# A gated mix of linear and softmax attention: branch A's normalising steps gathered into one iteration

## The chip, the cores and the metric

The kernel runs on one core of a Trainium2 chip. The core's engines work side by side: TensorE (PE, with its weight loads as PEld) for matrix products, VectorE (DVE), ScalarE (ACT) and GpSimd (POOL) for the rest, and SyncE (SP), whose queue issues the DMA transfers. Each engine works through its own list of instructions in order, and semaphores tie the lists together. The metric is the device time of one execution in microseconds (us), and the time given for a kernel is the median of its runs.

## The reference

The input x is 2048 tokens by 448 numbers, with 16 heads of 28 numbers each. Two attention branches are computed on the same x and mixed by a gate for each token:

```
g = sigmoid((x * gate_w).sum(-1))
out = g * A(x) + (1 - g) * B(x)

A: q, k, v = split(x @ wqkv); pq, pk = q @ w_phi, k @ w_phi         (per head)
   phi_q = [softmax(pq), softmax(-pq)]; phi_k = [softmax(pk), softmax(-pk)]
   kv = phi_k^T v; z = sum(phi_k); num = phi_q kv; den = phi_q z + 1e-6
   A = (num / den) @ wo
B: A = softmax(q k^T / sqrt(28)) v @ wo
```

So branch A is a linear attention with 56 features a head, and branch B a full softmax attention over all pairs of tokens.

## The kernel before, in words

Many factors of products are kept in two parts, a high part (the number rounded to TensorE's input format, F32R) and a low part (what the rounding left), and such a product is made in three passes. Tokens are tiled by 128, which gives 16 tiles; branch A's queries are also taken in 8 blocks of 256.

The program has three stretches. One loop of 44 iterations i computes branch A's keys, values and queries, and much of what branch B needs. After it branch B's attention runs block by block over all pairs, and then the results are joined. The change lies in the last half of that loop. There t = i is the tile of keys and values, q = i - 16 that of queries, y = q - 1 the step that A's output is at, and tb = y // 2 its block.

A block b of branch A takes these steps. `numer` makes its numerators and denominators on PE. `normalize1` copies the numerators from PSUM to a tile `oU` (ACT, L418) and gathers the denominators by a DMA (L420). `normalize2` adds the epsilon (DVE, L426), takes the reciprocals (L427), sends them to DRAM (L430) and spreads them over the partitions by four broadcast DMAs (L435). `normalize3` is the normalising product `oU * rs` (DVE, L441, 128x1024). `normalize4` makes the high parts (ACT, L448, two of 128x512) and the low parts (L449): the first by POOL, the second by DVE. `take_spread` then moves rows within the tile `oT` by four DMAs (L461), since `out_a` takes the output product in passes that need some rows in the partitions that stood empty. `out_a` (PE, tile `poa`) makes the output of one tile of tokens, and `out_a2` multiplies it by the gate (ACT, L638, tile `ga`) and sends it to DRAM (L639). In the iterations: numer(b) at y = 2b + 4, normalize2 at y = 2b + 5, normalize3 at y = 2b + 8, normalize4 and the moves at y = 2b + 9, out_a for the two tiles at y = 2b + 11 and 2b + 12.

Around these stand other steps of the same iterations. `mx_unit` is a unit of branch B's row maxima: PE multiplies keys and queries into two PSUM tiles `pmb` and `pmd` (L296), ACT copies the one (L303, tile `rl`), and DVE takes the maximum of both (L305, two instructions). Its PSUM tiles have two buffers up to y = 20, so that a unit's products wait until ACT and DVE have done with an earlier unit; from then on three buffers. `features1` and `features2` make the softmax features of the queries (DVE L476, L477, L492, L493; POOL L480, L482, L494; ACT L474, L485), `turn` transposes them on PE (`pft`, L558) and copies them from PSUM (ACT, L561, tile `fT`). The first three tiles of branch B's values are computed early, while A's are still running, into tiles `ve0` and `ve1`, which use buffers of the row-max copies (tags rl2 and rl3). At q = NT + 6, which is y = 21, two DMAs copy them (L921, L922; 512 KB and 256 KB) into the value tile `vb0`. Two iterations later row-max copies may use the buffer rl2 again, and so have to wait for that transfer.

PE, DVE, ACT and POOL run in the order in which the program is written. SP's order is set by a scheduler, except that transfers wrapped in `kept()` keep the order in which they are written among themselves. SP issues in order: a transfer that waits holds all those behind it.

Of the kernel before, what the change touches and what calls it, by code (L numbers as in the profile page):

```python
# [24 lines left out]
NT = S // P  # L25
# [10 lines left out]
def f32(ap):  # L36
    return ap.bitcast(F32)
# [3 lines left out]
def gated_mix_kernel(ctx, tc, xT, wqkB, wvB, wvA, wkAT, wqAT, phi, woA, woB,  # L41
# [7 lines left out]
    nc = tc.nc  # L49
# [124 lines left out]
    def take_acts():  # L174
        while acts:
            acts.pop(0)()

    def take_subs():
        while subs:
            subs.pop(0)()  # L180
# [229 lines left out]
    def kept(x, n=2):  # L410
        if n == 2:
            tc.stamp_issue_order_token(x.ins, "turns")
# [10 lines left out]
    def normalize2(pool, oU, den, nm, n, eps):  # L423

        if eps:
            nc.vector.tensor_scalar_add(den, den, EPS)  # L426
        nc.vector.reciprocal(den, den)  # L427
        rd = dr.tile([4, n * 512], F32, tag=f"rd{n}", name=f"rd{nm}", bufs=2)
        rs = pool.tile([P, n, 512], F32, tag="rs", name=f"rs{nm}", bufs=2)
        kept(nc.sync.dma_start(rd, den), n)  # L430
        if n == 1:
            nc.sync.dma_start(rs[:, 0, :], rd.unsqueeze(1).to_broadcast([4, 32, 512]))
            return oU, rs
        for j in range(4):
            kept(nc.sync.dma_start(rs[32 * j:32 * j + 32].rearrange("p n q -> p (n q)"),  # L435
                                   rd[j:j + 1].to_broadcast([32, n * 512])))
        return oU, rs

    def normalize3(oU, rs, n):

        (nc.gpsimd if n == 1 else nc.vector).tensor_mul(oU, oU, rs)  # L441
        return oU

    def normalize4(pool, oU, nm, n):

        o = pool.tile([P, n, 2, 512], F32R, tag="oT", name=f"oT{nm}", bufs=2)
        for k in range(n):
            (nc.scalar.copy if n == 2 else nc.gpsimd.tensor_copy)(o[:, k, 0, :], oU[:, k, :])  # L448
            (nc.vector if n == 2 and k == 1 else nc.gpsimd).tensor_sub(  # L449
                o[:, k, 1, :], oU[:, k, :], f32(o[:, k, 0, :]))  # L450
        if n == 2:
            spread.append(o)
        return [o[:, k] for k in range(n)]
# [3 lines left out]
    def take_spread():  # L457
        while spread:
            o = f32(spread.pop())
            for r in range(0, P, 32):  # L460
                kept(nc.sync.dma_start(  # L461
                    o[r + DH:r + 32].rearrange("p k i n -> p (k i n)")[:, :1792].rearrange(
                        "p (s n) -> p s n", n=256),
                    o[r:r + DH, 1, 1, 256:]))
# [34 lines left out]
    def take_exps(left=0):  # L499
        while len(exps) > left:  # L500
            exps.pop(0)()

    fk, va, fq, fT_of, num, oTs = {}, {}, {}, {}, {}, {}
# [108 lines left out]
    def load_split(w, nm):  # L612
        for i in range(2):
            nc.sync.dma_start(f32(w[:, i, :, :D]), w_d[nm][:, i])
# [21 lines left out]
    def out_a2(t):  # L636
        ga = ta.tile([P, D], F32, tag="ga", name=f"ga{t}", bufs=2)
        nc.scalar.mul(ga, po_of.pop(t)[:, :D], gate[:, t:t + 1])  # L638
        nc.sync.dma_start(ga_d[t // 4][:, t % 4], ga)  # L639
# [167 lines left out]
    for i in range(2 * NT + 12):  # L807
        t, q = i, i - NT
        y = q - 1
        tb = y // 2  # L810
        take_acts()
        if t < NT and t % 2 == 0:
            mx_unit()
            passes = (55 if t < NT - 4 else 44) + (4 if t >= 4 else 0)
            pace["n"] = 4 if t >= 4 else 0
            pace["at"] = [passes // 3, 2 * passes // 3] if t <= 10 else [passes // 2]
        if q in (0, 1):
            take_exps()
        if part_low:
            part_low.pop()()  # L820
        if q == 0:
            woA_s = weights(3, "woA_s")
            wvB_s = weights(2, "wvB_s")
            load_split(woA_s, "woA")
            load_split(wvB_s, "wvB")

        if t % 2 == 0 and 0 <= t - 4 < NT:
            kv_add(t - 4)
            kv_add(t - 3)
        if q == 2:  # L830
            bk_s.close()
            ta_s = ExitStack()
            ta = ta_s.enter_context(tc.tile_pool(name="ta", bufs=1, reuse_waits="tile"))
            KV = ta.tile([P, 512], F32, name="KV")
            woC_s = ta.tile([P, 2, D], F32R, name="woC_s")
            woC0 = wqA_s.rearrange("p i b n -> p (i b) n")[:, :7, D:]
            nc.sync.dma_start(f32(woC_s), w_d["woA"][:, 0, 1:3])
            nc.sync.dma_start(f32(woC0), w_d["woA"][:, 0, 0].rearrange("p (a n) -> p a n", n=64))
            kvT = kv_copy()
            early = [ta.tile([P, 2 - i, 512], F32, tag=f"rl{i + 2}", name=f"ve{i}", bufs=1) for i in range(2)]  # L840
            early = [e.rearrange("p t (h d) -> p t h d", d=32) for e in early]
            for e in early:
                nc.gpsimd.memset(e[:, :, :, 28:], 0.0)
                nc.gpsimd.memset(e[:, :, :, 28:29], 1.0)
            turn4.append("")
            take_exps()
        if t < NT:
            pk = ps_s(f"pk{t}")
            tok_major(pk, t, wkA_s, D, tick)
            fk[t] = features1(pk, f"k{t}", nc.gpsimd)  # L850
            take_exps(1)
        if 0 <= q < NT:
            pq = ps_s(f"pq{q}")
            tok_major(pq, q, wqA_s, D)
        if q == 0:
            fk[NT - 1] = features2(fk[NT - 1], f"k{NT - 1}")
        if q in (1, 2):
            fq[q - 1] = features2(fq[q - 1], f"q{q - 1}")
        if 0 <= q < NT:
            fq[q] = features1(pq, f"q{q}", nc.vector if 0 < q < 11 else nc.gpsimd)  # L860
        if 0 <= t - 1 < NT - 1:
            fk[t - 1] = features2(fk[t - 1], f"k{t - 1}")
        if 8 <= q < 11:
            value_b(q - 8)
        if q == NT + 5:
            ps_s_.close()
            ps = ps_s_.enter_context(tc.tile_pool(name="psv", bufs=1, space=PSUM, reuse_waits="tile"))
            psn[:] = 2, 3
            turn4.clear()
        if q == NT + 8:  # L870
            rl_at[:] = [(rlp, "rl"), (ta, "rl2")]
        if q in (0, 1) or q >= 11:
            mx_unit()
        if y >= 9 and y % 2 and tb - 4 < 8:
            oTs[tb - 4] = normalize4(ta, num.pop(tb - 4), f"a{tb - 4}", 2)
            take_spread()
        if y >= 4 and y % 2 == 0 and tb - 2 < 8:
            numer(tb - 2)
        if q > 0:
            take_exps(int(q < NT))  # L880
        if q == 3:
            kv_out(kvT)
        if q in (4, 5):
            spare_weights(q - 4)
        if 2 <= q - 1 < NT:
            fq[q - 1] = features2(fq[q - 1], f"q{q - 1}")
        take_subs()
        if t == 1:
            pair_load(0, 3)
        if y >= 8 and y % 2 == 0 and tb - 4 < 8:  # L890
            num[tb - 4] = normalize3(*num[tb - 4], 2)
        if t < NT:
            value_a(t)
            if t % 2 and t < NT - 4:
                proj_qk(NP + t // 2, ev)
                if t < 8:
                    part_low.append(part_high(t // 2))
        if q in (0, 1):
            proj_qk(NP + 6 + q, ev)
        take_lows()  # L900
        if 2 <= i < 6:
            fold(wqA_s, "q", i - 2)
        if q == 1:
            ev_s.close()
        if q == 1:
            gates()
        if y < 9 or y % 2:
            if y >= 2 and y - 2 < NT:
                turn(y - 2)
        if 0 <= y - 11 < NT:  # L910
            out_a(y - 11)
            out_a2(y - 11)
        if y >= 9 and y % 2 == 0 and y - 2 < NT:
            turn(y - 2)
        if q == NT + 2:
            bd_s.close()
            vb = [value_tile(0)]
        if q == NT + 6:
            for e in early:
                nc.gpsimd.memset(e[:, 0, 0:1, 29:30], 0.0)  # L920
            nc.sync.dma_start(vb[0][:, 0:2], early[0])  # L921
            nc.sync.dma_start(vb[0][:, 2:3], early[1][:, 0:1])  # L922
        if q - NT in (3, 4, 6, 7, 9):
            value_b(3 + (3, 4, 6, 7, 9).index(q - NT), (lambda i: i == 5 and mx_unit()) if q >= NT + 5 else None)
        if y >= 5 and y % 2 and tb - 2 < 8:
            num[tb - 2] = normalize2(ta, *num[tb - 2], f"a{tb - 2}", 2, True)
    rl_at.clear()
    ta_s.close()
    wp_s.close()
# [445 lines left out]
```

## Time and profile before

| | us |
|---|---|
| median of 3 runs | 1001.29 |
| their range | 1001.2 to 1002.0 |
| the profiled execution's own time | 1001.51 |
| its span in the profile | 999.7 |
| PE busy in the span | 991.4 |
| ACT busy | 807.4 |
| DVE busy | 666.3 |
| POOL busy | 231.7 |

The span is what the profiler sees between the first and the last instruction; 1.8 us of the profiled execution lie around it. The clock that TensorE was granted was 0.999 of full speed. Rows of the profile's views give a start and a duration in us, the engine, the line of the kernel, the operation, the tiles that it writes and reads, and in brackets how long the engine had been idle before it and what ended that. L12 is line 12 of the kernel. PE has the longest busy time, and the loop that the change touches lasts until about 331 us.

### The profile page before, as it was taken

To read this page: it belongs to the slowest core of one execution; us is meant where nothing else is said; L and a number is where in the kernel's file an instruction comes from. 1 tells how busy PE (TensorE), PEld (TensorE's weight loads), DVE (VectorE), ACT (ScalarE), POOL (GpSimd) and SP (SyncE) were. 2 spreads that over 40 slices of the span, in tenths; PEclk is the share of its full clock that TensorE was granted. 3 is DMA by queue.
4 is the path that set the end of the run, shared out by engine and by line. 5 is a ranking of instruction groups with operands and counts; after the bars stand their busy time and mean duration, and the time that the engine had idled before them with its cause. 6 is when DMAs were issued, how large, how long until landed. Compare 5 with 4: busy or idle time off the path is not lost.

```text
span 999.7 us, 18087 instructions
## 1 busy us (share of the span) xinstructions
PE 991.4 (99%) x6456; PEld 553.5 (55%) x6456; DVE 666.3 (67%) x1343; ACT 807.4 (81%) x1532; POOL 231.7 (23%) x214
## 2 busy tenths in 40 slices
PE   9999999999999999999999999999999999999998
PEld 8878878887777533333333333333334444455656
DVE  6567666888764588878888788888886544444202
ACT  5445555568855899999999999999999999979672
POOL 1265455668415111110120100102001011101010
PEclk9999999999999999999999999999999999999999
DMA  8976312412445732332524324443233354216231
GB/s 291 316 243 211 121 59 78 169 46 79 119 131 133 163 96 56 78 79 64 114 58 108 81 51 142 90 99 94 59 90 77 76 113 120 51 37 148 62 106 56
DMA packets 69170, 109.09 MB, mean 109 GB/s; under 512 B 18216, under 2 KB 29112, under 8 KB 69080
## 3 DMA queue, kind: packets, MB, share of 16 engines
q1 hardware_dynamic: 69080, 107.94, 40.0%
q8 instruction: 51, 0.84, 0.4%
q14 instruction: 39, 0.32, 0.1%
HBM read 74.33 MB, written 31.45 MB: 106 GB/s over the span
## 4 chain that ended last, share of the span: by engine, by line
PE 95%; DMA 2%; SPq 1%; DVE 1%; issue 1%; ACT 0%; POOL 0%; POOLq 0%; DVEq 0%; ACTq 0%
PE st L1040 28%; PE pv L1144 25%; PE pm L337 9%; PE pqk L118 6%; PE pva L136 4%; PE pk L136 4%; PE pq L118 4%; PE pob L118 3%; PE pvb L136 2%; PE poa L118 2%; PE pmb L296 2%; PE pft L558 1%; PE pqk L725 1%; PE pkv L512 1%; DMA oTa<-oTa 1%; PE poL L1182 1%
## 5 line engine op out<-in xcount | busy, mean ns | idle before, releaser
L1043 ACT ACTIVATE p<-st 128x512 f32<-128x512 f32 x1020 | 527.2, 638 | 25.9 <-PE st L1040 25.9
L348 DVE TENSOR_REDUCE part<-pm 128x1 f32<-128x512 f32 x450 | 287.3, 685 | 150.5 <-PE pm L337 150.5
L1040 PE MATMUL st<-qst,kst 128*128 128x512 f32 x1020 | 301.0, 423 | 0.4 <-DVE acc L1159 0.4
L1144 PE MATMUL pv<-p,vb 128*32 128x512 f32 x2048 | 263.7, 602 | 0.0
L1040 PEld LDWEIGHTS st<-qst,kst 128*128 128x128 f32 x1020 | 168.7, 187 | 99.6 <-ACT p L1043 45.0
L341 ACT ACTIVATE rl<-pm 128x512 f32<-128x512 f32 x200 | 124.3, 622 | 13.9 <-PE pm L337 12.4
L337 PEld LDWEIGHTS pm<-kc,qc 28*128 28x128 f32 x800 | 38.2, 181 | 167.7 <-issue 101.4
L441 POOL TENSOR_TENSOR oUb<-oUb,rsb 128x512 f32<-128x512 f32 x15 | 19.3, 1288 | 460.9 <-DMA rsb<-rdb 299.1
L345 DVE CUSTOM_DVE_ANT_0 rl<-pm,rl 128x512 f32<-128x512 f32 x150 | 102.0, 680 | 0.0
L337 PE MATMUL pm<-kc,qc 28*128 28x512 f32 x800 | 101.3, 495 | 0.0
L1144 PEld LDWEIGHTS pv<-p,vb 128*32 128x32 f32 x2048 | 47.3, 108 | 95.6 <-issue 89.5
L305 DVE CUSTOM_DVE_ANT_0 rl<-pmb,rl 128x512 f32<-128x512 f32 x112 | 72.0, 680 | 34.9 <-ACT rl L303 34.8
L303 ACT ACTIVATE rl<-pmd 128x1024 f32<-128x1024 f32 x56 | 57.5, 1027 | 17.9 <-issue 8.7
L118 PE MATMUL pqk<-XH,wB 128*128 128x512 f32 x192 | 59.3, 397 | 0.0
L662 ACT CAST ev<-pqk 128x512 fp32r<-128x512 f32 x28 | 16.0, 589 | 36.6 <-PE pqk L118 25.2
L118 PE MATMUL poa<-woA_s,oTa 128*128 128x448 f32 x128 | 38.0, 378 | 2.8 <-DMA oTa<-oTa 2.4
L118 PEld LDWEIGHTS pqk<-XH,wB 128*128 128x128 f32 x192 | 35.4, 188 | 8.5 <-issue 1.5
L1159 DVE SCALAR_TENSOR_TENSOR acc<-pob,gate,acc 128x448 f32<-128x448 f32 x12 | 8.2, 680 | 47.3 <-PE pob L118 47.3
L136 PE MATMUL pva<-wvA_s,XH 128*128 128x450 f32 x128 | 38.6, 375 | 0.0
L136 PE MATMUL pk<-wkA_s,XH 128*128 128x448 f32 x128 | 37.5, 374 | 0.0
L118 PE MATMUL pq<-wqA_s,XH 128*128 128x448 f32 x128 | 37.3, 374 | 0.0
L663 DVE TENSOR_TENSOR ev<-pqk,ev 128x512 fp32r<-128x512 f32 x28 | 19.0, 689 | 27.0 <-ACT ev L662 24.3
(169 smaller groups left out, 1172.6 us busy)
## 6 DMA issues: line engine op xcount, KB each, us to landing
qkd<-ev SPq DMA_DIRECT2D x28, 512.0 KB
qst<-qkd SPq DMA_DIRECT2D x64, 224.0 KB
kst<-qkd SPq DMA_DIRECT2D x64, 224.0 KB
od<-oTb SPq DMA_DIRECT2D x48, 112.0 KB
rsa<-rda SPq DMA_DIRECT2D x32, 128.0 KB
rsb<-rdb SPq DMA_DIRECT2D x15, 256.0 KB
kc<-qkd SPq DMA_DIRECT2D x64, 56.0 KB
gad<-ga SPq DMA_DIRECT2D x16, 224.0 KB
```

What stands on the lines that cost most here:

```text
L118: nc.tensor.matmul(d, l, r, start=i == 0, stop=i == len(todo) - 1)
L136: nc.tensor.matmul(dst[:, :n], l, r, start=i == 0, stop=i == len(todo) - 1, skip_group_check=True)
L296: nc.tensor.matmul((pb if j < 2 else pd)[:, j % 2, :], qc[js, qt * P:(qt + 1) * P], kc[js, :], start=True, stop=True, tile_position=(32 * ...
L303: nc.scalar.activation(rl, pd, AF.Relu)
L305: nc.vector.tensor_tensor_reduce(rl[:, i, :], pb[:, i, :], rl[:, i, :], 1.0, LOWEST, ALU.add, ALU.max, part[:, col + i:col + i + 1])
L337: nc.tensor.matmul(pm[j], mxs[("qc", gq)][js, qt * P:(qt + 1) * P], mxs[("kc", g, kb)][js, :], start=True, stop=True, tile_position=(32 * ...
L341: nc.scalar.activation(rl, pm[kb], AF.Relu if kb < 3 else AF.Copy)
L345: nc.vector.tensor_tensor_reduce(r, pm[j], r, 1.0, LOWEST, ALU.add, ALU.max, part[:, col + j:col + j + 1])
L348: nc.vector.tensor_reduce(part[:, col + j:col + j + 1], pm[j], AX.X, ALU.max)
L1040: nc.tensor.matmul(st, kst_of[(gq // NQ, kt // 4)][:, j, (kt % 4) * P:(kt % 4 + 1) * P], qst_of[gq][:, j, :], start=True, stop=True)
L1043: nc.scalar.activation(p, st, AF.Exp, scale=SCALE)
L1144: nc.tensor.matmul(pv[32 * j:32 * j + 32, :], vb[kt // 8][:, kt % 8, 4 * g + j, :], pt[j], start=kt == 0, stop=kt == NT - 1, tile_position ...
```

## The change

Three edits. In `normalize4` both low parts of branch A's blocks are made by DVE (before: one by POOL). `normalize3` is moved to stand ahead of `mx_unit` in its iteration, and `normalize4` with `take_spread` is moved from the next iteration, y = 2b + 9, into the same one, y = 2b + 8, behind `out_a2` and ahead of `turn`. The transfer of the early values is moved to the end of its iteration, behind `normalize2`, and is wrapped in `kept()`.

```diff
@@ normalize4
-            (nc.vector if n == 2 and k == 1 else nc.gpsimd).tensor_sub(
+            (nc.vector if n == 2 else nc.gpsimd).tensor_sub(
                 o[:, k, 1, :], oU[:, k, :], f32(o[:, k, 0, :]))
@@ the loop over i
+        if y >= 8 and y % 2 == 0 and tb - 4 < 8:
+            num[tb - 4] = normalize3(*num[tb - 4], 2)
         if q in (0, 1) or q >= 11:
             mx_unit()
-        if y >= 9 and y % 2 and tb - 4 < 8:
-            oTs[tb - 4] = normalize4(ta, num.pop(tb - 4), f"a{tb - 4}", 2)
-            take_spread()
...
-        if y >= 8 and y % 2 == 0 and tb - 4 < 8:
-            num[tb - 4] = normalize3(*num[tb - 4], 2)
...
             out_a(y - 11)
             out_a2(y - 11)
+        if y >= 8 and y % 2 == 0 and tb - 4 < 8:
+            oTs[tb - 4] = normalize4(ta, num.pop(tb - 4), f"a{tb - 4}", 2)
+            take_spread()
         if y >= 9 and y % 2 == 0 and y - 2 < NT:
             turn(y - 2)
...
-        if q == NT + 6:
-            for e in early:
-                nc.gpsimd.memset(e[:, 0, 0:1, 29:30], 0.0)
-            nc.sync.dma_start(vb[0][:, 0:2], early[0])
-            nc.sync.dma_start(vb[0][:, 2:3], early[1][:, 0:1])
         if q - NT in (3, 4, 6, 7, 9):
             value_b(3 + (3, 4, 6, 7, 9).index(q - NT), (lambda i: i == 5 and mx_unit()) if q >= NT + 5 else None)
         if y >= 5 and y % 2 and tb - 2 < 8:
             num[tb - 2] = normalize2(ta, *num[tb - 2], f"a{tb - 2}", 2, True)
+        if q == NT + 6:
+            for e in early:
+                nc.gpsimd.memset(e[:, 0, 0:1, 29:30], 0.0)
+            kept(nc.sync.dma_start(vb[0][:, 0:2], early[0]))
+            kept(nc.sync.dma_start(vb[0][:, 2:3], early[1][:, 0:1]))
```

PE's order is the same in both programs. On DVE, from the iteration y = 14 on (block 3; `rl32` to `rl34` are row-max units, `fsumq` the feature sums, `dena5` block 5's denominators, `oUa3` and `oTa3` block 3's numerators and parts; of each unit's L305 the first of its rows is shown, and two small steps ahead of unit 32 are left out), the order before:

```order
L305 ISA rl32_2892,part_94<-pmb32_2886,rl32_2892 128x512
L492 TENSOR_REDUCE fsumq14_2920<-feat2_466 128x32
L493 RECIPROCAL fsumq14_2920<-fsumq14_2920 128x32
L441 TENSOR_TENSOR oUa3_2596<-oUa3_2596,rsa3_2693 128x1024
L305 ISA rl33_2959,part_94<-pmb33_2953,rl33_2959 128x512
L449 TENSOR_TENSOR oTa3_2963<-oUa3_2596,oTa3_2963 128x512
L492 TENSOR_REDUCE fsumq15_2973<-feat3_467 128x32
L493 RECIPROCAL fsumq15_2973<-fsumq15_2973 128x32
L426 TENSOR_SCALAR dena5_2917<-dena5_2917 128x32
L427 RECIPROCAL dena5_2917<-dena5_2917 128x32
L305 ISA rl34_3019,part_94<-pmb34_3013,rl34_3019 128x512
```

and with the change:

```order
L441 TENSOR_TENSOR oUa3_2597<-oUa3_2597,rsa3_2693 128x1024
L305 ISA rl32_2893,part_94<-pmb32_2887,rl32_2893 128x512
L492 TENSOR_REDUCE fsumq14_2921<-feat2_466 128x32
L493 RECIPROCAL fsumq14_2921<-fsumq14_2921 128x32
L449 TENSOR_TENSOR oTa3_2940<-oUa3_2597,oTa3_2940 128x512 x2
L305 ISA rl33_2968,part_94<-pmb33_2962,rl33_2968 128x512
L492 TENSOR_REDUCE fsumq15_2973<-feat3_467 128x32
L493 RECIPROCAL fsumq15_2973<-fsumq15_2973 128x32
L426 TENSOR_SCALAR dena5_2918<-dena5_2918 128x32
L427 RECIPROCAL dena5_2918<-dena5_2918 128x32
L441 TENSOR_TENSOR oUa4_2747<-oUa4_2747,rsa4_2858 128x1024
L305 ISA rl34_3020,part_94<-pmb34_3014,rl34_3020 128x512
```

Block 3's product now stands ahead of unit 32's maximum, its two low parts ahead of unit 33's, and block 4's product, which came later, ahead of unit 34's.

On ACT at the same place (`ga3` the gated output, `fT6` the transposed features, `rl33` a row-max copy), before:

```order
L638 ACTIVATE ga3_2937<-poa3_2925,gate_84 128x448
L561 COPY fT6_2940<-pft12_0_2941 128x4x128
L561 COPY fT6_2940<-pft12_4_2942 128x4x128
L303 ACTIVATE rl33_2959<-pmd33_2954 128x1024
L448 CAST oTa3_2963<-oUa3_2596 128x512 x2
L485 ACTIVATE feat3_467<-feat3_467 128x16x56
```

and with the change:

```order
L638 ACTIVATE ga3_2937<-poa3_2925,gate_84 128x448
L448 CAST oTa3_2940<-oUa3_2597 128x512 x2
L561 COPY fT6_2949<-pft12_0_2950 128x4x128
L561 COPY fT6_2949<-pft12_4_2951 128x4x128
L303 ACTIVATE rl33_2968<-pmd33_2963 128x1024
L485 ACTIVATE feat3_467<-feat3_467 128x16x56
```

The two high parts now stand ahead of the copies of the transposes and of the row-max copy.

On SP around y = 21 (`rda7` and `rsa7` block 7's reciprocals and their broadcasts, `oTa6` block 6's rows, `qp3_1` queries that are loaded, `vb0` the value tile), before:

```order
L430 DMA rda7_3257<-dena7_3177 128x32
L639 DMA gad2_71<-ga9_3291 128x448
L921 DMA vb0_3129<-ve0_2060 128x1024
L435 DMA rsa7_3258<-rda7_3257 32x1024 x4
L461 DMA oTa6_3304<-oTa6_3304 4x7x256 x4
L639 DMA gad2_71<-ga10_3325 128x448
L922 DMA vb0_3129<-ve1_2061 128x512
L185 DMA qp3_1_3355<-qkd_68 28x512 x4
L639 DMA gad2_71<-ga11_3383 128x448
```

and with the change:

```order
L430 DMA rda7_3257<-dena7_3178 128x32
L639 DMA gad2_71<-ga9_3291 128x448
L185 DMA qp3_1_3356<-qkd_68 28x512 x2
L435 DMA rsa7_3258<-rda7_3257 32x1024 x4
L461 DMA oTa6_3294<-oTa6_3294 4x7x256 x4
L639 DMA gad2_71<-ga10_3325 128x448
L925 DMA vb0_3129<-ve0_2060 128x1024
L926 DMA vb0_3129<-ve1_2061 128x512
L185 DMA qp3_1_3356<-qkd_68 28x512 x2
```

The two transfers of the early values now stand behind the broadcasts, block 6's rows and the output `ga10`, and two of the four query loads stand ahead of the broadcasts.

## The prediction

> **What bounds the kernel now.** I read the page's busy shares first, then the stage that the change touches by stretches of time, then TensorE's waits in it, then the chain of waits. PE is busy 99% of the span:
>
> ```profile
> PE 991.4 (99%) x6456; PEld 553.5 (55%) x6456; DVE 666.3 (67%) x1343; ACT 807.4 (81%) x1532; POOL 231.7 (23%) x214
> ```
>
> So an edit off PE can only return the time in which PE stands idle. The edited iterations run from about 220 to 310 us of the span. Columns: stretch, length, busy us (and instructions) of PE, PEld, DVE, ACT, POOL, then clock, DMA share, GB/s:
>
> ```profile
> 220.00:250.00 30.00, 29.82 (x232) 24.33 (x238) 25.56 (x49) 23.43 (x40) 25.70 (x18) 1.00 0.24 66
> 250.00:268.00 18.00, 17.53 (x172) 13.28 (x164) 15.94 (x32) 16.12 (x30) 10.26 (x9) 1.00 0.40 119
> 268.00:310.00 42.00, 39.72 (x234) 30.51 (x218) 23.55 (x59) 23.81 (x34) 4.16 (x6) 1.00 0.40 120
> ```
>
> PE's idle time is 0.18 + 0.47 + 2.28 = 2.93 us: the ceiling of any gain here, 0.29% of the run. DVE is 89% busy in the middle stretch. What PE waits for from 195 to 332 us (total, times, longest):
>
> ```profile
> PE poa L118 <- DMA oTa<-oTa: 2.4, 3, 1.3
> PE poa L118 <- ACT vb L794: 0.2, 1, 0.2
> PE poa L118 <- ACT rl L303: 0.2, 1, 0.2
> ```
>
> All but 0.4 us is A's output product waiting for the moved rows, and PE's timeline places it (start, duration, idle before):
>
> ```profile
> 264.83 0.65 PE L118 MATMUL poa<-woA_s,oTa 128*128 128x448 f32 x2 [0.39 <-DMA oTa<-oTa]
> ...
> 283.45 0.65 PE L118 MATMUL poa<-woA_s,oTa 128*128 128x448 f32 x2 [1.31 <-DMA oTa<-oTa]
> ...
> 304.40 0.44 PE L118 MATMUL poa<-woA_s,oTa 128*128 128x448 f32 x1 [0.75 <-DMA oTa<-oTa]
> ```
>
> These are blocks 3, 5 and 7: 0.39 + 1.31 + 0.75 = 2.45 us. The chain of waits (start, length, what) tells what made them late:
>
> ```profile
> 257.42 1.74 POOL oTa L449
> 259.18 0.65 SPq L461
> ...
> 262.41 3.32 DMA rda<-dena
> ...
> 271.42 2.87 DMA rda<-dena
> ...
> 277.03 0.58 SPq L420
> ...
> 277.72 0.65 SPq L461
> ...
> 279.75 3.57 DMA oTa<-oTa
> ...
> 297.45 1.15 DVE oTa L449
> ...
> 298.66 0.65 SPq L461
> ```
>
> Block 3's rows left when GpSimd had finished its low part. SP takes its transfers in turn, and from there a ring leads on: the rows of block 3, block 5's reciprocals (262.41), their broadcasts, and by way of block 6's (271.42) to the rows of block 5 at 277.72, directly behind a denominator's move. Block 7's rows left when VectorE's low part ended.
>
> **The change, term by term.** One block's product, high and low parts and move now end one iteration sooner: the product stands ahead of the row-max unit, the low parts are both on DVE, and the rows are sent in the same iteration. The view of the tile (min/median/max ns, first and last start):
>
> ```profile
> L449 DVE TENSOR_TENSOR oTa<-oUa,oTa x8: 822/1001/1224, 224.0 to 297.4; 128x512 fp32r<-128x512 f32 x8
> L449 POOL TENSOR_TENSOR oTa<-oUa,oTa x8: 1289/1302/1757, 224.2 to 296.7; 128x512 fp32r<-128x512 f32 x8
> ```
>
> Removed: eight GpSimd parts of about 1.3 us. Added: eight on DVE. The longest, 1.22, is the upper bound of one; the lower follows with DVE's rows.
>
> *The gain.* Block 7's DVE part is no longer behind the row maximum of an iteration later; its rows leave at least 2 us before 298.66, which covers 0.75. Block 3's leave when two DVE parts are done, about 257.7 instead of 259.18, which is 1.5 sooner and covers 0.39. Block 5's rows cannot pass the broadcasts and the denominator's move ahead of them on SP (277.03), so they gain only what the ring gains: between nothing and 1.2 us. The two short waits (0.4) lie in later iterations; what delays PE earlier covers them. Gain: 2.45 at least if PE loses 1.31 earlier anyway or the ring gains it, 2.85 with the short ones.
>
> *What it costs on DVE.* The place is 250 to 263 us. DVE there, then GpSimd, blocks 3 and 4 (start, duration), and DVE's reciprocal step once undisturbed (269.90):
>
> ```profile
> 252.74 0.68 DVE L305 CUSTOM_DVE_ANT_0 rl<-pmb,rl 128x512 f32<-128x512 f32 x1
> ...
> 254.74 1.16 DVE L441 TENSOR_TENSOR oUa<-oUa,rsa 128x1024 f32<-128x1024 f32 x1
> ...
> 256.57 0.69 DVE L305 CUSTOM_DVE_ANT_0 rl<-pmb,rl 128x512 f32<-128x512 f32 x1
> ...
> 257.18 0.83 DVE L449 TENSOR_TENSOR oTa<-oUa,oTa 128x512 fp32r<-128x512 f32 x1
> ...
> 259.70 1.63 DVE L426 TENSOR_SCALAR dena<-dena 128x32 f32<-128x32 f32 x1 [0.26 <-DMA dena<-oUa]
> ...
> 262.18 0.69 DVE L305 CUSTOM_DVE_ANT_0 rl<-pmb,rl 128x512 f32<-128x512 f32 x1
> ...
> 262.79 1.22 DVE L441 TENSOR_TENSOR oUa<-oUa,rsa 128x1024 f32<-128x1024 f32 x1
> ...
> 269.90 0.18 DVE L426 TENSOR_SCALAR dena<-dena 128x32 f32<-128x32 f32 x1 [2.80 <-DMA dena<-oUa]
> ```
>
> ```profile
> 254.99 2.47 POOL L494 TENSOR_TENSOR feat<-feat,fsumq 128x896 f32<-128x896 f32 x1 [1.70 <-ACT fT L561]
> ...
> 259.58 1.71 POOL L494 TENSOR_TENSOR feat<-feat,fsumq 128x896 f32<-128x896 f32 x1 [0.43 <-DVE fsumq L493]
> ```
>
> A low part with GpSimd at rest may take half a whole product, 1.22 / 2 = 0.6; I take 0.83, the row of block 3 itself (257.18), which is also the shortest of the eight.
>
> PE's next row-max product writes a buffer that the row maximum (L305) before the last must have left. PE's rows that depend on it:
>
> ```profile
> 254.16 0.49 PE L296 MATMUL pmb<-kp,qp 28*128 28x512 f32 x2
> ...
> 257.86 0.49 PE L296 MATMUL pmb<-kp,qp 28*128 28x512 f32 x2
> ...
> 262.84 0.50 PE L296 MATMUL pmb<-kp,qp 28*128 28x512 f32 x2
> ```
>
> The last L305 ends at 262.87, and PE's product stands at 262.84: no slack at all. Ahead of that L305 the change puts block 3's second low part (0.83) and block 4's product, which ran after it at 262.79 (1.22). From 250 on DVE rested only 0.26 us in these rows. So L305, and with it PE, comes 0.83 + 1.22 - 0.26 = 1.8 us later. The same sum along the way: block 3's product moves ahead of the first L305 (1.16 later; it ended at 253.42, and PE came at 254.16, 0.7 after it), two low parts ahead of the second (257.26 + 0.83 + 0.83 = 258.9, against 257.86 needed: a wait of 1.05). These are not added to the 1.8; they are how it is reached.
>
> Bounds of this cost: below, 0.9, if a low part without GpSimd takes 0.6 and half of L426's fall from 1.63 to the 0.18 of 269.90 is won because the GpSimd part at 257.42 is gone (0.6 + 1.22 - 0.26 - 0.7). Above, 3.3: GpSimd's feature products (L494) are still there, and the rows show the two engines taking turns: L494 lasted 2.47 beside the product instead of 1.71, and L426 1.63, ending just after L494 did. One more such hold is worth 1.63 - 0.18 = 1.4 us. The row speaks of 1.8; I add 0.2 for ScalarE below.
>
> The Trainium skill, page "SBUF — State Buffer", section "Who interferes with whom", has a rule for this: a VectorE instruction with two SBUF inputs and a GpSimd instruction share a port pair that the one issued first keeps for its whole length, while the other stands still. The trace agrees (L426's 1.63 beside L494's 1.71). It speaks against putting more two-input work on VectorE here, but equally the GpSimd part that is removed can no longer hold anything; by the rule alone the sum lies anywhere between the bounds.
>
> In the later stretch, 268 to 310, DVE is busy 23.55 of 42 us and GpSimd 4.16, so blocks 5 to 7 cost nothing: DVE's idle time hides them; if it did not, 0.83 each. Blocks 0 to 2 fall in 220 to 250, where PE has its own long products and the ceiling shows waits of 0.18; the same cover.
>
> *ScalarE.* The high parts (L448) now stand ahead of the transposes' copies on even iterations:
>
> ```profile
> 253.92 1.07 ACT L561 COPY fT<-pft 128x512 f32<-128x512 f32 x2
> ...
> 255.94 1.15 ACT L448 CAST oTa<-oUa 128x512 fp32r<-128x512 f32 x2
> ```
>
> The copies come 1.15 us later in their iteration, and the row-max copy behind them too, ending near 257.0, still ahead of PE's 257.86. PE's numerators and transposes wait for the copies with little in hand: 0 to 0.5, taken as 0.2.
>
> *The early values.* Their first transfer, what follows it on SP, and a late row-max copy of ACT:
>
> ```profile
> 285.24 0.56 SPq L921 DMA_DIRECT2D vb<-ve x1
> 285.88 2.28 SPq L435 DMA_DIRECT2D rsa<-rda x4
> 288.27 2.70 SPq L461 DMA_DIRECT2D oTa<-oTa x4
> ```
>
> ```profile
> 295.08 1.03 ACT L303 ACTIVATE rl<-pmd 128x1024 f32<-128x1024 f32 x1
> ```
>
> Both early transfers now stand behind the broadcasts, block 6's rows and one result's move. The four broadcasts and four rows take 2.28 + 2.70 = 5.0 us to issue. Nothing holds the broadcasts until 285.88 any more, so the first transfer leaves near 290 and both have landed by 293 to 293.6, an estimate from the 3.57 that the late rows of block 5 took. Two query loads take the transfer's place ahead of the broadcasts; their data have long been there, and they are issued in the time in which SP waited for 285.24, so the broadcasts start no later. The row-max copy that reuses the early values' buffer is the one at 295.08: 1.5 to 2 us in hand, so the term is nothing; without this cover it costs up to 1.
>
> *Sum.* Against the profiled execution's 1001.51 (span 999.7): -2.85 + 1.8 + 0.2 = -0.85, so 1000.66. That execution lies 0.2 above the median of the runs, 1001.29; against the median it is **1000.5**. Behind the stage PE goes on with the same work, 99% busy as over the whole span, and passes the difference on to the end.
>
> **The rivals.** *A, DVE keeps its turn:* the parts take 0.6 each, GpSimd's relief frees L426, and the new waits stay at 0.6 or less: -2.85 + 0.6 = -2.25, near 998.9. For it: GpSimd's busy 10.26 of 18 us falls by 1.7 at least. Against: the zero slack at 262.84, and that with so little delay on PE block 5 is held by the ring again, so A needs the ring 0.7 or more sooner. *B, slower by turn-taking:* at the product and the low parts of blocks 3 and 4 DVE is held by L494 or GpSimd's feature differences. The price is the 1.4 us of such a hold each; with 1.8 + 0.2 and two or three of them the new waits are 4.8 to 6.2, and the run 1003.2 to 1004.6, say 1003.9. It turns the sign from 2.85 us of new waits on. For it: L426 and one L494 above are stretched already. Against: they took turns before as well, and GpSimd has two instructions fewer there. *C, the ring gets longer and the change does not do what it says:* the second low part comes ahead of L426, so block 5's reciprocals leave SP up to 1.3 after 262.41, and the rows of block 5 after 277.72 by as much. PE then waits at 283.45 as before, only later: +0.8 to +1.3 there, against 1.15 won behind it (0.75 + 0.4): near 1001.3. For it: SP's order, which the change leaves as it was there. Against: block 3's rows leave SP 1.5 sooner.
>
> **How the numbers follow.** Chances: forecast 0.48 (own range 999.4 to 1001.4), A 0.21, B 0.18, C 0.13. What can be told from no change here is about 0.2%, 2.0 us: faster is below 999.3, slower above 1003.3. A gives 0.20 of faster and the forecast's lower end 0.02; B gives 0.16 of slower and the upper tails of the others 0.02. The range, 998.7 to 1002.9, holds the forecast, C, nearly all of A and the mild end of B.
>
> **What would show it.** Right: the waits at 264.83, 283.45 and 304.40 for moved rows gone or under 0.2; new waits of PE for the row maximum (pmb on DVE's L305) between 254 and 265, near 2 us together; the DVE parts at 0.6 to 0.9 where GpSimd rests. A: no such waits. B: parts or products of 1.6 us and more beside L494. C: 1.2 or more still before block 5's output. The forecast is wrong if PE's idle time after 310 us changes, or if the row-max copy near 295 waits for the early values.

## The result, and the profile after

The changed kernel takes 1003.45 us (median of 17 runs, 1001.02 to 1004.98) against 1001.63 for the kernel before (17 runs, 1001.20 to 1002.65). The ratio is 1.0015, with a 95% interval of 1.0008 to 1.0022: about 1.5 us slower by this ratio, 1.8 by the medians. The forecast was 1000.5 within 998.7 to 1002.9, so both its sign and its range missed. The profiled execution took 1003.78.

What PE waits for in the changed kernel between 195 and 335 us (total, times, longest):

```profile
PE pmd L296 <- DVE part L305: 2.9, 4, 1.4
PE poa L118 <- DMA oTa<-oTa: 0.2, 1, 0.2
```

The waits for moved rows, 2.4 us before, are all but gone. Waits for the row maxima have taken their place, and they are larger. The three longest stand at blocks 3 and 4:

```profile
257.32 0.50 PE L296 MATMUL pmd<-kp,qp 28*128 28x512 f32 x2 [1.44 <-DVE part L305]
...
262.57 0.50 PE L296 MATMUL pmd<-kp,qp 28*128 28x512 f32 x2 [1.07 <-DVE part L305]
...
268.11 0.50 PE L296 MATMUL pmd<-kp,qp 28*128 28x512 f32 x2 [0.26 <-DVE part L305]
```

The same stretches of time as before (length, busy us of PE, PEld, DVE, ACT, POOL, then clock, DMA share, GB/s):

```profile
220.00:250.00 30.00, 29.83 (x221) 24.60 (x220) 29.65 (x50) 23.38 (x39) 19.64 (x14) 1.00 0.23 65
250.00:268.00 18.00, 15.34 (x139) 11.05 (x137) 17.08 (x31) 13.06 (x21) 8.18 (x5) 1.00 0.33 92
268.00:310.00 42.00, 41.70 (x246) 32.24 (x247) 25.13 (x65) 26.46 (x42) 0.87 (x4) 1.00 0.43 124
```

PE's idle time went from 2.28 to 0.30 us in the last stretch and from 0.47 to 2.66 in the middle one, where DVE is now 95% busy. In the first, DVE rose from 25.56 to 29.65 of 30 us.

Idle time alone does not give the balance, since PE's ends are modelled. Starts of the same instructions do. First a copy on ACT that stands ahead of every edit, in the kernel before:

```profile
215.87 0.53 ACT L794 COPY ve<-pvb 128x448 f32<-128x448 f32 x1 [1.64 <-PE pvb L118]
```

and in the changed kernel, followed by PE's starts of the outputs that waited before (blocks 3, 5 and 7):

```profile
216.49 0.53 ACT L794 COPY ve<-pvb 128x448 f32<-128x448 f32 x1 [1.64 <-PE pvb L118]
```

```profile
269.38 0.65 PE L118 MATMUL poa<-woA_s,oTa 128*128 128x448 f32 x2
...
286.61 0.64 PE L118 MATMUL poa<-woA_s,oTa 128*128 128x448 f32 x2 [0.19 <-DMA oTa<-oTa]
...
306.69 0.68 PE L118 MATMUL poa<-woA_s,oTa 128*128 128x448 f32 x2
```

Before they stood at 264.83, 283.45 and 304.40, so the lag is 4.55, 3.16 and 2.29. Of it 0.62 was there before the first edited instruction: it stems from the first 8 us of the span, where PE's first eight products (L725) took 2.88 us instead of 2.06. PE therefore lost 4.55 - 0.62 + 0.39 = 4.32 us up to block 3's output (the 0.39 is the old wait that fell away there), and won 0.39, then 1.39, then 0.87: 2.65 in all. The net is 1.67 in this execution, close to the medians' 1.8.

SP sent the rows of blocks 3, 5 and 7 at these times in the changed kernel (start, duration of the four issues; the second row is block 5's reciprocals):

```profile
261.36 2.64 SPq L461 DMA_DIRECT2D oTa<-oTa x4
...
264.60 0.42 SPq L430 DMA_DIRECT2D rda<-dena x1
...
280.89 2.66 SPq L461 DMA_DIRECT2D oTa<-oTa x4
...
297.39 2.79 SPq L461 DMA_DIRECT2D oTa<-oTa x4
```

Before they stood at 259.18, 262.41, 277.72 and 298.66. So block 3's and block 5's rows left later than before, and only block 7's sooner.

Most of the 4.32 can be read from DVE's rows of blocks 3 and 4. In the kernel before, DVE came to them here:

```profile
250.80 0.56 DVE L476 TENSOR_REDUCE extq<-pcq 128x16 f32<-128x448 f32 x1
```

and in the changed kernel its rows are these (start, duration; the second L449 row is the later one of the pair by itself):

```profile
253.04 0.56 DVE L476 TENSOR_REDUCE extq<-pcq 128x16 f32<-128x448 f32 x1
...
254.04 1.67 DVE L441 TENSOR_TENSOR oUa<-oUa,rsa 128x1024 f32<-128x1024 f32 x1
...
258.29 0.35 DVE L493 RECIPROCAL fsumq<-fsumq 128x32 f32<-128x32 f32 x1
258.56 2.74 DVE L449 TENSOR_TENSOR oTa<-oUa,oTa 128x512 fp32r<-128x512 f32 x2
259.11 2.19 DVE L449 TENSOR_TENSOR oTa<-oUa,oTa 128x512 fp32r<-128x512 f32 x1
...
263.82 0.12 DVE L426 TENSOR_SCALAR dena<-dena 128x32 f32<-128x32 f32 x1
263.97 0.35 DVE L427 RECIPROCAL dena<-dena 128x32 f32<-128x32 f32 x1
264.24 2.59 DVE L441 TENSOR_TENSOR oUa<-oUa,rsa 128x1024 f32<-128x1024 f32 x1
266.75 0.68 DVE L305 CUSTOM_DVE_ANT_0 rl<-pmb,rl 128x512 f32<-128x512 f32 x1
...
267.36 0.68 DVE L305 CUSTOM_DVE_ANT_0 rl<-pmb,rl 128x512 f32<-128x512 f32 x1
```

GpSimd's rows beside them:

```profile
258.79 1.95 POOL L494 TENSOR_TENSOR feat<-feat,fsumq 128x896 f32<-128x896 f32 x1 [2.28 <-DVE fsumq L493]
264.05 1.70 POOL L494 TENSOR_TENSOR feat<-feat,fsumq 128x896 f32<-128x896 f32 x1 [3.30 <-DVE dena L426]
```

DVE's L493 releases GpSimd's feature product (L494). The first low part is running by then; L494 gets in behind it, between the two parts, and the second part stands until L494 ends at 260.74. Block 4's product comes 0.19 us after the next L494 has begun and stands for 1.4. Behind each stands the row maximum that PE needs. DVE was late when it came to these rows, too: by 2.24 us at L476, or 1.6 without the 0.62 of the start, from the iterations of blocks 0 to 2.

### The profile page after: what moved, and what is told of

It reads as the page before. It is cut to its first block, busy times and chain, and to the rows that moved or that the text cites. A ratio compares the mean times of both kernels' runs of the same rounds, so it can differ in the third digit from the quotient of the medians.

```text
span 1002.0 us, 18060 instructions
## 1 busy us (share of the span) xinstructions
PE 993.5 (99%) x6456; PEld 555.6 (55%) x6456; DVE 676.6 (68%) x1351; ACT 807.6 (81%) x1532; POOL 221.0 (22%) x206
## 4 chain that ended last, share of the span: by engine, by line
PE 95%; DVE 3%; DMA 1%; SPq 1%; issue 0%; ACT 0%; POOL 0%; DVEq 0%; POOLq 0%
PE st L1040 28%; PE pv L1144 25%; PE pm L337 9%; PE pqk L118 6%; PE pva L136 4%; PE pk L136 4%; PE pq L118 3%; PE pvb L136 3%; PE pob L118 3%; PE poa L118 3%; PE pmb L296 2%; PE pqk L725 1%; PE pft L558 1%; PE pkv L512 1%; PE poL L1182 1%; PE pvb L118 1%
## 5 line engine op out<-in xcount | busy, mean ns | idle before, releaser
L305 DVE CUSTOM_DVE_ANT_0 rl<-pmb,rl 128x512 f32<-128x512 f32 x112 | 72.1, 681 | 30.8 <-ACT rl L303 30.8
```

The costliest lines, as they stand in the source:

```text
L305: nc.vector.tensor_tensor_reduce(rl[:, i, :], pb[:, i, :], rl[:, i, :], 1.0, LOWEST, ALU.add, ALU.max, part[:, col + i:col + i + 1])
```

## The experiments

All times are medians of 11 runs unless said; the kernel before took 1001.7 to 1001.8 beside them.

| run | what differs from which kernel | us | ratio to before, 95% |
|---|---|---|---|
| one_low | changed, both low parts in one instruction | 1000.79 | 0.9991 (0.9982 to 1.0000) |
| no_featprod | changed, L494 of eight tiles left out | 1000.20 | 0.9984 (0.9975 to 0.9993) |
| early_back | changed, third edit undone (5 runs) | 1007.41 | 1.0053 (1.0040 to 1.0065) |
| one_low_prod_after | one_low, product behind the row-max unit | 1002.55 | 1.0007 (0.9998 to 1.0015) |
| early_only | before, third edit alone | 1001.91 | 1.0001 (0.9992 to 1.0010) |
| low_gpsimd | changed, first edit undone | 1000.58 | 0.9991 (0.9982 to 0.9999) |
| low_only | before, first edit alone | 1002.79 | 1.0007 (0.9999 to 1.0016) |
| prod_first | one_low, products in other places | 1002.88 | 1.0009 (1.0001 to 1.0018) |
| one_low_b4 | one_low, block 4 in another order | 1000.50 | 0.9985 (0.9976 to 0.9994) |
| low_gpsimd_b4 | low_gpsimd, the same | 1000.80 | 0.9989 (0.9980 to 0.9998) |
| changed_again | the changed kernel | 1003.33 | 1.0010 (1.0001 to 1.0018) |

### One instruction for both low parts

```diff
-            (nc.vector if n == 2 else nc.gpsimd).tensor_sub(
-                o[:, k, 1, :], oU[:, k, :], f32(o[:, k, 0, :]))
+            if n == 1:
+                nc.gpsimd.tensor_sub(o[:, k, 1, :], oU[:, k, :], f32(o[:, k, 0, :]))
+        if n == 2:
+            nc.vector.tensor_sub(o[:, :, 1, :], oU, f32(o[:, :, 0, :]))
```

> Both low parts of a block as one DVE instruction of 128x2x512 instead of two of 128x512; all else as in the changed kernel. Theory 1 (turn-taking: GpSimd's feature product L494 starts between the two parts and the second is held until it ends, 2.19 us in the changed kernel's rows): the low parts of a block take about 1.25 us instead of 2.73, L494 starts after them, PE's delay of 4.9 us in 229 to 263 us falls by about 1.5, and the time by as much, to about 1002.0. Theory 2 (the DVE and ACT work put ahead of the row maxima is what costs, wherever GpSimd is): within 0.3 of the changed kernel's 1003.45.

Measured: 1000.79, 2.7 us below the changed kernel, more than theory 1 expected; against the kernel before it lies at the edge of the noise. DVE does the same arithmetic at the same place; what went is the gap between the parts. It went in blocks 1 and 2 as well, which is why more came back than one block's 1.5: DVE's L476 ahead of block 3's product (its L478) now stands at 252.04, 1.45 sooner than in the changed kernel when both are counted from the copy ahead of all edits (216.94 here). In this kernel's DVE and GpSimd rows at block 3 (its L452 is the low part, its L496 the feature product, since lines were added):

```profile
257.57 1.16 DVE L452 TENSOR_TENSOR oTa<-oUa,oTa 128x1024 fp32r<-128x1024 f32 x1
...
261.82 2.44 DVE L441 TENSOR_TENSOR oUa<-oUa,rsa 128x1024 f32<-128x1024 f32 x1
```

```profile
257.80 2.49 POOL L496 TENSOR_TENSOR feat<-feat,fsumq 128x896 f32<-128x896 f32 x1 [2.28 <-DVE fsumq L495]
261.48 1.70 POOL L496 TENSOR_TENSOR feat<-feat,fsumq 128x896 f32<-128x896 f32 x1 [1.19 <-DVE fsumq L495]
```

The low parts take 1.16 instead of 2.74, and now it is GpSimd that waits (2.49 for a product that takes 1.70 alone), where nothing needs it soon. Block 4's product is still held, 2.44. PE's waits are down to this:

```profile
PE pmd L296 <- DVE part L305: 0.8, 3, 0.3
```

### The feature product left out

```diff
-        nc.gpsimd.tensor_mul(f2, f2, sm.unsqueeze(3).to_broadcast([P, H, 2, DH]))
+        if nm[0] == "k" or int(nm[1:]) < 8:
+            nc.gpsimd.tensor_mul(f2, f2, sm.unsqueeze(3).to_broadcast([P, H, 2, DH]))
```

> Leaves out the product that normalises the softmax features of the query tiles 8 to 15 (L494 on GpSimd); all else as in the changed kernel. Theory 1: with nothing on GpSimd at these places no DVE part is held: two low parts 1.2 us together, products 1.2 except where L480 and L482 run, PE's new delay falls from 4.9 to about 2, the time to about 1000.5. Theory 2: the added DVE work is still there, 1003 or more.

Measured: 1000.20, as theory 1 had it. DVE's rows of blocks 3 and 4 with L494 absent:

```profile
255.37 1.22 DVE L449 TENSOR_TENSOR oTa<-oUa,oTa 128x512 fp32r<-128x512 f32 x2
...
259.87 1.16 DVE L441 TENSOR_TENSOR oUa<-oUa,rsa 128x1024 f32<-128x1024 f32 x1
```

The pair takes 1.22 and block 4's product 1.16, both with DVE's program as in the changed kernel. The products of blocks 1 to 3, beside L480 and L482, still take 1.72. The two runs together show that the loss is the holding by L494, not the DVE work as such: with the work kept and this holding gone, the time is 1.5 us below that before instead of 1.5 above. This kernel leaves out a step that the result needs, so it is no gain to be had.

### The early values back at their old place

```diff
-            kept(nc.sync.dma_start(vb[0][:, 0:2], early[0]))
-            kept(nc.sync.dma_start(vb[0][:, 2:3], early[1][:, 0:1]))
```

(and the block moved back ahead of `value_b`, without `kept`).

> Only the third edit undone: the early values' transfer back at its old place and outside the kept order. If it neither costs nor gives (the prediction's term of nothing): 1003.2 to 1003.7. If the transfer behind the broadcasts is what frees the rows of blocks 6 and 7: about 0.8 slower, 1004.2. If it delays the row-max copy near 295 us: up to 1 faster.

Measured: 1007.41, 4 us slower than the changed kernel and far outside all three expectations. SP's rows say why:

```profile
270.88 0.56 SPq L921 DMA_DIRECT2D vb<-ve x1
271.53 2.29 SPq L435 DMA_DIRECT2D rsa<-rda x4
...
278.80 0.56 SPq L922 DMA_DIRECT2D vb<-ve x1
281.08 2.74 SPq L435 DMA_DIRECT2D rsa<-rda x4
```

In the kernel before, the first transfer stood ahead of block 7's broadcasts; here the scheduler has put it ahead of block 5's, two blocks sooner, and the second one ahead of block 6's. SP waits for it, and block 5's broadcasts leave at 271.53, where they left at 265.74 before. PE pays for it twice:

```profile
280.19 0.50 PE L296 MATMUL pmd<-kp,qp 28*128 28x512 f32 x2 [1.57 <-DVE part L305]
...
290.25 0.68 PE L118 MATMUL poa<-woA_s,oTa 128*128 128x448 f32 x2 [1.47 <-DMA oTa<-oTa]
```

So the transfer's place is not given by where it is written: moving other code moved it.

### The third edit alone

```diff
+        if q == NT + 6:
+            for e in early:
+                nc.gpsimd.memset(e[:, 0, 0:1, 29:30], 0.0)
+            kept(nc.sync.dma_start(vb[0][:, 0:2], early[0]))
+            kept(nc.sync.dma_start(vb[0][:, 2:3], early[1][:, 0:1]))
```

(at the end of the iteration, in the kernel before, in place of its own block).

> The kernel before with the third edit alone: the early values' transfer at the end of its iteration and in the kept order. In the run without it (1007.4) the transfers stood two iterations sooner on SP and held the broadcasts; in the kernel before they stand where they held one set of broadcasts only, for blocks whose rows are not late by it. Theory a (the edit only keeps the other two from being scheduled badly): 1001.3 to 1002.0, no change. Theory b (it frees SP's ring by itself): the waits at 283.45 and 304.40 shrink and the time is 0.8 to 2 less, about 1000.3.

Measured: 1001.91, no difference (0.9992 to 1.0010): theory a. The three old waits are all still there (0.24, 1.35 and 0.81).

### The first edit undone, and alone

Undone in the changed kernel:

```diff
-            (nc.vector if n == 2 else nc.gpsimd).tensor_sub(
+            (nc.vector if n == 2 and k == 1 else nc.gpsimd).tensor_sub(
```

> The first edit undone: the first low part on GpSimd again; the new places and the early transfer as in the changed kernel. Theory 1 (what costs is the second of two DVE parts, held by L494): one DVE part of 0.6 to 0.9 goes ahead of L494, 2.1 of PE's 4.9 us of delay go, about 1001.3, unless GpSimd's part, now behind L494 in its queue, comes too late for the output product. Theory 2 (GpSimd's own queue is then the limit): its part ends about 3 us later than the DVE pair does now, block 3's rows of the output wait, 1002.5 to 1003.5.

Measured: 1000.58, theory 1's side and lower than its 1001.3. The other two edits without the first are 1.1 us faster than before, just clear of the noise (0.9982 to 0.9999), and the first costs about 2.8 on top. One DVE part directly behind L493 takes 0.63, L494 follows, and GpSimd's part comes last, ending 3.4 us after DVE's began, soon enough: PE's only wait for moved rows is block 5's, 1.23 in this execution.

Alone in the kernel before, at its old place:

> The kernel before with the first edit alone: both low parts on DVE, at their old place an iteration later. There the pair stands behind a row maximum and not behind the feature sums, so L494 does not start between the two: DVE pair 1.2 to 1.4, PE later by 0.83 - 0.26 = 0.6 at 262.84, block 3's wait of 0.39 gone, the ring as before: 1001.2 to 1002.0. If the pair is held here too: 1003.

Measured: 1002.79, between the two cases and nearer to the second. At the old place the pair is held less (2.18, 1.42 and 1.58 in blocks 1 to 3), but the waits of before stay (1.24 and 0.81 for blocks 5 and 7), and some for ScalarE come in. So the first edit gives nothing of its own; that it costs something is not shown (0.9999 to 1.0016).

### Where the product stands

First behind the row-max unit:

```diff
-        if y >= 8 and y % 2 == 0 and tb - 4 < 8:
-            num[tb - 4] = normalize3(*num[tb - 4], 2)
         if q in (0, 1) or q >= 11:
             mx_unit()
+        if y >= 8 and y % 2 == 0 and tb - 4 < 8:
+            num[tb - 4] = normalize3(*num[tb - 4], 2)
```

> One low part as in one_low, and the normalising product behind the row-max unit instead of ahead of it; the high and low parts stay in the same iteration. Theory 1: the DVE work ahead of the row maxima is at most 0.4 us more than before the change and no instruction is held for a whole L494, so the new delay is 0.6 to 1.0 and the old waits (2.85) are gone as in the changed kernel: 999.3 to 1000.3, faster than both. Theory 2: only the product's 1.2 us is won against one_low: 1000.8 if one_low is at 1002.0, and 1002.2 if it is at 1003.4.

Measured: 1002.55; both theories missed. ScalarE's row at block 1 and PE's waits in this kernel:

```profile
230.81 1.14 ACT L448 CAST oTa<-oUa 128x512 fp32r<-128x512 f32 x2 [1.68 <-DVE oUa L441]
```

```profile
PE pft L560 <- ACT fT L563: 1.4, 2, 1.0
PE pmd L296 <- ACT rl L303: 0.8, 1, 0.8
PE poa L118 <- ACT fT L563: 0.5, 1, 0.5
```

The high parts (L448) wait for the later product, the copies of the transposes queue up behind them on ScalarE, and PE waits for the copies. The waits have changed engine. It follows, though no run tried it by itself, that the product has to be early for ScalarE and must not be in front of a row maximum for long.

Then ahead of the feature extremes for blocks 0 to 3, and behind the unit for block 4:

```diff
+        if 8 <= y < 16 and y % 2 == 0:
+            num[tb - 4] = normalize3(*num[tb - 4], 2)
         if t < NT:
             pk = ps_s(f"pk{t}")
...
+        if y == 16:
+            num[4] = normalize3(*num[4], 2)
         if y >= 4 and y % 2 == 0 and tb - 2 < 8:
             numer(tb - 2)
```

> One low part as in one_low; the product of blocks 0 to 3 ahead of the feature extremes (L476), so that L480 and L482 do not run beside it, block 4's behind the row-max unit, so that it is not issued right behind the start of L494; blocks 5 to 7 as changed. Theory 1: products 1.2 us everywhere, 0.5 + 1.2 us less of DVE time ahead of the row maxima than in one_low, of which PE sees 0.5 to 0.9: about 1000.0. If ScalarE's queue is the limit instead (high parts and copies of transposes later, as with the product behind the unit, 1002.55): 1001.5 or more.

Measured: 1002.88, a miss. DVE's rows of blocks 1 and 2 there:

```profile
227.74 2.59 DVE L441 TENSOR_TENSOR oUa<-oUa,rsa 128x1024 f32<-128x1024 f32 x1
...
239.06 2.59 DVE L441 TENSOR_TENSOR oUa<-oUa,rsa 128x1024 f32<-128x1024 f32 x1
```

The new place avoids L480, but it is the one directly behind L493, L426 and L427, so L494 is just running: 2.59 instead of 1.59 and 1.33 as in one_low. That is one more case of the same holding. PE waits 1.35 at 232.66 for the row maximum behind block 1's product, and 1.70 at 268.00 for copies behind block 4's high parts; what each did to the time was not separated.

### Block 4 alone, and the changed kernel again

```diff
+        if y == 16:
+            num[4] = normalize3(*num[4], 2)
         if y >= 4 and y % 2 == 0 and tb - 2 < 8:
             numer(tb - 2)
...
             turn(y - 2)
+        if y == 16:
+            oTs[4] = normalize4(ta, num.pop(4), "a4", 2)
+            take_spread()
```

(and the two general places leave out y = 16).

> one_low with block 4 alone in another order: its product behind the row-max unit and its parts behind the copies of the transposes. In one_low this product took 2.44 us, held by a feature product that had started 0.3 us before it. Theory 1: it takes 1.2, the row maximum of unit 34 no longer stands behind it, and PE gains 0.3 to 0.7 on one_low: 1000.1 to 1000.5, with runs below the fastest of the kernel before. Theory 2 (what is left is ScalarE's order): no gain, 1000.8 or more.

> low_gpsimd with the same edit to block 4. Theory 1: the product, 2.37 us there, takes 1.2: 0.3 to 0.7 less, near 1000.1. Theory 2: GpSimd's low part of block 4 and SP's ring bind, no gain: 1000.6 or more.

> The changed kernel, word for word, beside the two. If its time is the same here as at first: 1003.0 to 1003.8, so that the differences from the runs above hold; its DVE rows show the pair of low parts held (2.7 us) in every block from 1 to 3.

Measured: 1000.50, 1000.80 and 1003.33. Block 4's product takes 1.32 in the first and 1.22 in the second, as theory 1 had it, but the times cannot be told from those of one_low and low_gpsimd. What is left in PE's waits is of another kind, in the first of them:

```profile
PE pmd L296 <- DVE part L305: 1.5, 3, 0.9
PE poa L118 <- DMA oTa<-oTa: 0.5, 1, 0.5
```

one_low_b4 has the lowest median of the kernels that leave nothing out: 0.15% below the kernel before (0.06 to 0.24%), and 2.8 us below the changed one beside it. The changed kernel's repeat agrees with its first time, and its pairs of low parts are held for 2.73 in blocks 1 to 3 again.

## Why the prediction was wrong

- **The gain** came out in size: 2.85 us forecast, 2.65 measured, at the places named, with 0.19 of block 5's 1.31 left. In part that was luck. Block 7's rows left SP 1.9 sooner without the 0.62 of the start (forecast: at least 2). But block 3's left at 261.36, 2.18 later than before and not 1.5 sooner, and block 5's 3.17 later. PE did not wait for them because it had lost more than that itself. The forecast had allowed for this at block 5 ("if PE loses 1.31 earlier anyway"), not at block 3. Where PE is less late, in low_gpsimd, block 5's wait is 1.23.
- **The place** was right: PE waits for DVE's L305 between 254 and 268.
- **The size of the new waits** was wrong, and it turned the sign: 2.0 forecast (1.8 for DVE, 0.2 for ScalarE), 4.32 measured. Of the 0.2 nothing is seen: PE's waits in the changed kernel name DVE and the moved rows alone. The term that failed is "block 3's second low part (0.83) and block 4's product (1.22)". The 0.83 was the row of a part that stood 0.2 us for the end of one L494 (254.99 + 2.47) and then ran ahead of GpSimd's own part; two parts one behind the other were taken as twice that, 1.66, and took 2.74, of which the second alone 2.19, far above the 1.22 named as the upper bound of one. The product took 2.59. Block 3's product, moved beside L480 and L482, took 1.67 instead of 1.16. That is 1.1 + 1.4 + 0.5 = 3.0 more, of which L426, 0.12 instead of 1.63, gave 1.5 back. L494 was named as what might hold DVE, and one such hold was priced at 1.4 in the upper bound, but the sum took none of them. The written orders showed the two held instructions directly behind L493 and L427, so the holds could have been read off: L493 is what releases L494.
- **What those terms leave over**: the last row maximum of the stretch starts at 267.36 instead of 262.18: 5.18 later, or 4.56 without the 0.62. By the terms above DVE should have added 1.8 + 3.0 - 1.5 = 3.3 from L476 on, and its rows show 2.9. The other 1.6 it had brought along.
- **Blocks 0 to 2 at nothing, behind PE's long products**, is where the 1.6 comes from, and is the second term that failed. That PE was busy there said nothing of DVE, which was already busy for 25.56 of 30 us: the pair of blocks 1 and 2 takes 2.73 each, DVE is 29.65 of 30 us busy, and ScalarE's row-max copy at 249.99 before stands 1.23 later after, 0.6 of it beyond the 0.62 at the start.
- **"The GpSimd part that is removed can no longer hold anything"** was right and beside the point. What the rule of the Trainium skill left open, who is next, decided: the engines alternate, and two short DVE instructions leave a gap that one long one does not. That is shown by one_low. The row given as agreeing with the rule, L426's, has only one such input; the row of a two-input instruction was L494's 2.47 beside block 3's product.
- **Rival B** is the mechanism that happened, at 0.18. The time lies in its 1003.2 to 1004.6. Its price, 4.8 to 6.2 us of new waits, was a little high: 4.32 at PE, and a net of 1.7 instead of 2.6. It counted two or three holds at blocks 3 and 4; two were there, and those of blocks 0 to 2, which it did not name, besides. It was right that the sign turns at 2.85. **A** comes nearest in the kernel without L494's holds: no_featprod, 1000.20, where A had 998.9 (by its own sum, 1001.29 - 2.25, it is 999.0). **C**'s longer ring is there: block 5's reciprocals leave SP at 264.60, 2.19 later than before. Its wait at block 5 is not, since PE came later still.
- **The early values** at nothing: right for that edit alone (early_only), and the row-max copy that shares the buffer (298.23 in the changed kernel) shows no wait. But the term was incomplete: with the other two edits made, the old form of the transfer costs 4 us, since the scheduler then places it elsewhere. The edit is needed for the other two.
- **The move itself** (the second edit with the third) is worth 1.1 us of gain over before: low_gpsimd. Why the runs of the changed kernel spread over 4 us, where those of one_low spread over 1.4, was not settled. Both its profiles show the same holds of the low parts and of block 4's product, but they are of executions of 1003.78 and 1004.46; none of the executions near 1001 was profiled, so turns that fall otherwise in those are neither shown nor excluded.

## What to carry to other kernels

Before moving two-input SBUF work to VectorE, look which of its own instructions releases GpSimd work, and keep such work from standing close behind that one. Where it must stand there, make it a single long instruction that starts before GpSimd does, since a gap between two short ones is enough for GpSimd to get in. A long one that comes after GpSimd has begun is held all the same: one_low's product of block 4 took 2.44. A duration from a row is that of its neighbourhood: a part that took 0.83 at the end of one L494 took 2.19 at the start of another and 0.63 with nothing in its way. And a transfer that a scheduler places can move when other code moves, so look for its new place on the queue even when its own lines are unchanged.

## What the runs showed of the hardware

The two engines alternate. In the changed kernel DVE's second low part was ready behind its first without a pause (block 3's high parts had ended on ScalarE at 256.88), yet GpSimd's waiting L494 went in between, and the part lasted 2.19 us instead of 0.63 to 0.69: so in blocks 0 to 3 of both its profiles. As one instruction of 128x1024 the same work took 1.16 to 1.23 in blocks 1 to 3 beside the same L494, which then lasted 2.49 to 2.67 instead of 1.70; in block 0, where L494 had begun 0.4 before it, it took 2.40. The Trainium skill, page "SBUF — State Buffer", section "Who interferes with whom", says that whoever issues first keeps the shared ports for the whole instruction; the trace agrees, and adds that an engine that waits comes next even when the other has its next instruction ready. With one tile as input the picture is mixed. DVE's sums over the features (L492) took 1.07 to 1.09 both beside GpSimd's work and without it. L426, which also reads one tile, was held: 1.63 beside an L494 that had begun 0.12 before it, against 0.12 to 0.18 throughout with L494 left out.

Profiles also differ by the start: the copy at 215.87, ahead of all edits, came 0.62 later in the changed kernel's profile, and over all the kernels here it lies between 215.62 and 216.94. Whether the program or the single execution sets this is open; the two profiles of the changed kernel have 216.49 and 216.63. With effects of 1 to 2 us, two profiles have to be laid against each other from there, not from zero.
